# An adaLN, H3 and SwiGLU block: k's planes stored and loaded in order of use, first taps by halves, a quarter of the DFT matrix moved up

## The chip, the core and the metric

The kernel runs on one core of a Trainium2 chip. That core has a matrix engine (TensorE, PE; its weight loads are listed apart as PEld), three engines for elementwise work (VectorE or DVE, ScalarE or ACT, GpSimd or POOL), an engine that issues transfers (SyncE, SP), and 16 DMA engines that move data between the device memory and the on-chip memories. Each engine works through its own list of instructions in order and waits at an instruction until what it needs is there. The metric is the device time of one execution in microseconds (us).

## What is computed

One block with batch 1, S = 2048 tokens, D = 512 channels, F = 1792, all in float32. The core of the reference, shortened:

```python
mod = (silu(c) @ w_mod)            # six vectors sa, ca, ga, sb, cb, gb
h = layernorm(q) * (1 + ca) + sa
k_shift[t] = sum(k[t - i] * shift_k[:, i] for i in range(4))   # causal, per channel
kv = k_shift * v
y = irfft(rfft(pad(kv)) * rfft(pad(ssm_k)))[:S] + kv * ssm_D   # long causal convolution
x = q + ga * (h * y)
h = layernorm(x) * (1 + cb) + sb
out = x + gb * ((silu(h @ w_gate) * (h @ w_up)) @ w_down)
```

The change concerns only the first lines: how k, v and the DFT matrix come in, and how k_shift is made for the first two quarters of the channels.

## The kernel before

The channels are cut into four chunks of 128 (0 to 3). For every chunk the kernel makes kv = k_shift * v, transforms it and the filter ssm_k along time by a DFT of several steps (64 x 64 products with the matrix e_fwd, transposes of 32 x 32 blocks, small products with a matrix wc), multiplies the spectra and transforms back. This first stage takes about the first 125 us of the profile; behind it come the output products of the convolution, the norms, and then the SwiGLU part, which is matrix products on PE to the end.

The order of all work is written out by hand: a list of calls from line 1152 on, each of which appends its instructions to the engines that it names; instructions stay in that order on each engine, and the framework adds the waits. Tiles come from numbered buffers: a string of digits per kind (SLOTS, line 52) says which buffer each allocation takes. "e8" are eight buffers of 128 x 2048 numbers, for k, v, filter and tap results and for the DFT matrix ("er", line 235); "ps" are four pairs of PSUM banks. A tile in a used buffer waits for the last readers of the old one. All loads go out on SP in the order of the calls. The framework has eight semaphores for them, taken in turn: a load waits until the load eight places ahead of it has landed.

What the steps of the text use:

- Chunk 0 takes a path of its own, so that PE has work soon. Its k comes as "planes", 19 blocks of 128 x 128: plane j holds tokens with remainder j - 3 modulo 16, channels on partitions, preceded by three shifted ones for the taps; 20 small numbers per partition (taps of all chunks, c) stand ahead of them in the same tile (load_k0, line 163). The load has two pieces: the small numbers and planes 0 to 10 (714 KB), and planes 11 to 18 (512 KB).
- Chunk 0's first half of the tokens: four diagonal matrices of the taps (diag, line 180, "dg") are multiplied with the planes on PE (x0_taps, line 186, called for planes from 4 on and then from 0 on, planes 0 to 10 in all) and with v (x0_mul, line 196, DVE) into x00. Its second half: p_tap0 and p_tap (lines 204 and 208, DVE) make the taps on planes 8 to 18 elementwise into "u", p_mul (line 212, POOL and DVE) multiplies with v, and p_turn (line 216) transposes on PE; ACT copies the result into x01.
- Chunks 1 to 3 come with channels on partitions (load_k, load_v, lines 155 and 230). tap0 (line 243, ACT) makes the first tap of a whole chunk, tap (line 247, DVE) adds one of the other three, times_v (line 263) multiplies.
- load_e(q) (line 237) loads a quarter of the DFT matrix, x_first(c, q) (line 283) and k_first(c, q) (line 297) are the first products of chunk c with it: 8 matmuls, and a copy on ACT into X or kt. x_first(0, 0) and (0, 1) read x00, (0, 3) and (0, 2) read x01. swap_x and k_swap (DVE) transpose, x3 and product3 are the next products ("px" and "pk").
- warm(n) (line 136) runs n products on PE whose result nobody reads.

Of the kernel before, what the change touches and what calls it, by code (L numbers as in the profile page):

```python
# [42 lines left out]
def adaln_h3_swiglu(ctx, tc, q, k0, v0, kT, vT, ssm, dskip, wgu, wdn, wmod, e_fwd, e_inv, w_c, out):  # L43
# [8 lines left out]
    SLOTS = {  # L52
        "e8": "501234671063724603267137537135173135157137157137105637501657305617503657",
        "b16": "0123450224520214352",
# [99 lines left out]

    def load_k(b):
        kt = e8([P, S], F32, f"kt{b}")
        sp.dma_start(kt, kT[(b - 1) * P : b * P, :])
        kv[b] = [kt]

# [3 lines left out]
    def load_k0(h):  # L163

        if h == 0:
            t = head["t"] = b16("k0", (P, NS + (J + KS - 1) * P))
            head["k"] = t[:, NS:].rearrange("p (j m) -> p j m", m=P)
        m = NS + (J // 2 + KS - 1) * P
        r = slice(m, None) if h else slice(0, m)
        sp.dma_start(head["t"][:, r], k0[:, r])  # L170

    def load_v0(h):
        if h == 0:
            head["v"] = e8([P, 2, J // 2, P], F32, "v0")
        sp.dma_start(head["v"][:, h], v0[h])
# [4 lines left out]
    def diag(t, e=act):  # L180

        if t == 0:
            head["d"] = k2([P, KS, P], F32, "dg")
        scaled(e, head["d"][:, t], ident, head["t"][:, t : t + 1])

    def x0_taps(o):

        head["x", o] = bank("kvt")
        for jj in range(4):
            for t in range(KS):  # L190
                pe.matmul(
                    head["x", o][:, jj * P : (jj + 1) * P], head["k"][:, 4 * o + jj + KS - 1 - t],
                    head["d"][:, t], start=(t == 0), stop=(t == KS - 1),
                )
# [8 lines left out]

    def p_tap0(e=act):
        head["u"] = r4([P, J // 2, P], F32, "u0")
        scaled(e, head["u"], head["k"][:, J // 2 + KS - 1 :], head["t"][:, 0:1])

    def p_tap(t, h, e=dve):
        u, j = head["u"][:, 4 * h : 4 * h + 4], J // 2 + KS - 1 - t + 4 * h
        e.scalar_tensor_tensor(u, head["k"][:, j : j + 4], head["t"][:, t : t + 1], u, op0=ALU.mult, op1=ALU.add)  # L210
# [31 lines left out]

    def tap0(b, e=act):
        u = U[b] = e8([P, S], F32, f"u{b}")
        scaled(e, u, kv[b][0], shk_sb[:, b, 0:1])

    def tap(b, t):
        u = U[b]
        dve.scalar_tensor_tensor(
            u[:, t:], kv[b][0][:, : S - t], shk_sb[:, b, t : t + 1], u[:, t:], op0=ALU.mult, op1=ALU.add  # L250
        )

# [900 lines left out]
    load_k0(0)  # L1153
    load_k0(1)
    diag(0, e=act)
    diag(1, e=act)
    warm(7)
    diag(2, e=dve)
    small_in(e=act)
    silu_c()  # L1160
    load_k(1)
    p_tap0(e=dve)
    load_v0(0)
    p_tap(1, 0, e=dve)
    load_v0(1)
    load_k(2)
    load_dskip()
    p_tap(1, 1, e=dve)
    diag(3, e=act)
    x0_taps(1)  # L1170
    tap0(1, e=act)
    p_tap(2, 0, e=dve)
    p_tap(2, 1, e=dve)
    x0_taps(0)
    p_tap(3, 0, e=dve)
    p_tap(3, 1, e=dve)
    warm(5)
    tap(1, 1)
    tap0(2, e=act)
    x0_mul(0)  # L1180
    x0_mul(1)
    load_e(0)
    p_mul(0, e=pool)
# [575 lines left out]
```

## Time and profile before

| what | us |
|---|---|
| median of three runs (lowest, highest) | 566.36 (566.36, 566.46) |
| the profiled execution, its own time | 566.24 |
| span of that profile | 564.5 |
| busy: PE, PEld | 552.7, 431.1 |
| busy: DVE, ACT, POOL | 441.5, 288.7, 317.7 |

The profile is of one execution; its span runs from the first instruction to the last and is 1.74 us shorter than that execution's time. "Busy" counts instructions that run, not the waits. Names such as "kvt<-dg,k" mean: written tile, read tiles; "x64" is a count, and one product of float32 numbers is two matmul instructions. A bracket behind a row is the idle time of that engine just before it and what ended it. The chain of waits goes back from the last instruction, at each step to what released it; all else waited for something that was not last. Nearly every instruction has line 39, a helper, so rows are told apart by their tiles.

### The profile page before, as it was taken

To read this page: it belongs to the slowest core of one execution; us is meant where nothing else is said; L and a number is where in the kernel's file an instruction comes from. 1 tells how busy PE (TensorE), PEld (TensorE's weight loads), DVE (VectorE), ACT (ScalarE), POOL (GpSimd) and SP (SyncE) were. 2 spreads that over 40 slices of the span, in tenths; PEclk is the share of its full clock that TensorE was granted. 3 is DMA by queue.
4 is the path that set the end of the run, shared out by engine and by line. 5 is a ranking of instruction groups with operands and counts; after the bars stand their busy time and mean duration, and the time that the engine had idled before them with its cause. 6 is when DMAs were issued, how large, how long until landed. Compare 5 with 4: busy or idle time off the path is not lost.

```text
span 564.5 us, 9861 instructions
## 1 busy us (share of the span) xinstructions
PE 552.7 (98%) x3880; PEld 431.1 (76%) x3880; DVE 441.5 (78%) x602; ACT 288.7 (51%) x444; POOL 317.7 (56%) x298
## 2 busy tenths in 40 slices
PE   9899999898999999999999999999999999999997
PEld 9766456358788888888888888887888888888886
DVE  5989999998889666767567579858686868686766
ACT  3898889734664444434643556243434343434330
POOL 2359746899447966657978667550606061616110
PEclk9999999999999999999999999999999999999999
DMA  8998998991215655982897530544343434343304
GB/s 334 401 406 305 334 245 168 340 240 61 74 43 200 197 199 182 259 263 40 252 334 306 204 131 1 188 182 173 122 160 124 161 127 158 127 165 133 160 1 149
DMA packets 52544, 107.99 MB, mean 191 GB/s; under 512 B 19345, under 2 KB 34065, under 8 KB 46482
## 3 DMA queue, kind: packets, MB, share of 16 engines
q1 hardware_dynamic: 52498, 107.36, 56.3%
q8 instruction: 30, 0.49, 0.4%
q14 instruction: 16, 0.13, 0.1%
HBM read 72.74 MB, written 34.61 MB: 190 GB/s over the span
## 4 chain that ended last, share of the span: by engine, by line
PE 85%; DVE 9%; DMA 3%; ACT 1%; issue 1%; POOL 0%; SPq 0%; ACTq 0%; DVEq 0%
PE a L39 23%; PE dn L39 15%; PE c L39 12%; PE b L39 7%; PE da L39 6%; PE g L39 4%; PE s L39 4%; PE dc L39 3%; PE y L39 3%; DVE xs L39 3%; DVE X L39 2%; PE pk L39 2%; PE iv L39 2%; DMA er<-in_e_fwd 2%; DVE K L39 2%; PE px L39 1%
## 5 line engine op out<-in xcount | busy, mean ns | idle before, releaser
L39 PE MATMUL a<-op,wsum 128*128 128x512 f32 x432 | 109.9, 390 | 0.0
L39 PEld LDWEIGHTS a<-op,wsum 128*128 128x128 f32 x432 | 81.0, 188 | 17.5 <-ACT p L39 0.4
L39 PE MATMUL dn<-wd,acts 128*128 128x512 f32 x336 | 84.8, 389 | 0.0
L39 PEld LDWEIGHTS dn<-wd,acts 128*128 128x128 f32 x336 | 63.1, 188 | 13.1
L39 ACT COPY p<-a 128x512 f32<-128x512 f32 x50 | 29.4, 587 | 57.3 <-PE a L39 57.3
L39 DVE TENSOR_TENSOR x<-x,dn 128x512 f32<-128x512 f32 (+1 forms) x65 | 43.3, 671 | 13.2 <-PE dn L39 12.9
L39 POOL TENSOR_TENSOR wa<-ws,wa 128x512 fp32r<-128x512 f32 (+1 forms) x28 | 32.0, 1164 | 26.6 <-ACT wa L39 26.6
L39 POOL TENSOR_TENSOR tb<-wds 128x256 f32<-128x256 f32 x12 | 8.9, 744 | 62.4 <-DVE wds L39 62.4
L39 DVE TENSOR_TENSOR b<-r,c 128x512 f32<-128x512 f32 x24 | 16.7, 696 | 32.3 <-ACT sg L39 32.3
L39 ACT COPY r<-a 128x512 f32<-128x512 f32 x24 | 14.1, 587 | 53.7 <-PE a L39 53.6
L39 POOL TENSOR_TENSOR wsum<-sr,wsum 128x512 fp32r<-128x512 f32 x28 | 40.1, 1455 | 0.0
L39 PE MATMUL c<-op,wsum 128*128 128x512 f32 x156 | 39.6, 389 | 0.0
L39 PE MATMUL c<-op,wa 128*128 128x512 f32 x156 | 39.6, 389 | 0.0
L39 PE MATMUL b<-op,wa 128*128 128x512 f32 x144 | 36.5, 389 | 0.0
L39 POOL TENSOR_TENSOR wd<-wds,wd 128x512 fp32r<-128x512 f32 x14 | 18.3, 1329 | 30.4 <-ACT wd L39 30.4
L39 PEld LDWEIGHTS c<-op,wsum 128*128 128x128 f32 x156 | 29.3, 188 | 6.1
L39 PEld LDWEIGHTS c<-op,wa 128*128 128x128 f32 x156 | 29.3, 188 | 6.1
L39 POOL TENSOR_TENSOR s<-s,bcs 128x512 f32<-128x512 f32 x26 | 32.9, 1284 | 1.0
L39 DVE TENSOR_TENSOR x<-x,da 128x512 f32<-128x512 f32 x48 | 32.7, 681 | 0.9 <-PE da L39 0.9
L39 PEld LDWEIGHTS b<-op,wa 128*128 128x128 f32 x144 | 27.0, 188 | 5.6
L39 DVE TENSOR_TENSOR xs<-pk,xs 128x1024 f32<-128x1024 f32 x24 | 27.7, 1210 | 2.3 <-PE pk L39 2.2
L39 ACT ACTIVATE sg<-a 128x512 f32<-128x512 f32 x26 | 15.6, 599 | 22.5 <-PE a L39 22.5
(199 smaller groups left out, 1284.5 us busy)
## 6 DMA issues: line engine op xcount, KB each, us to landing
ds<-wsum SPq DMA_DIRECT2D x12, 1024.0 KB, 8.7
wsum<-ds SPq DMA_DIRECT2D x12, 1024.0 KB, 6.4
dw<-wa SPq DMA_DIRECT2D x12, 768.0 KB, 5.8
wa<-dw SPq DMA_DIRECT2D x12, 768.0 KB, 4.4
ws<-in_wgu SPq DMA_DIRECT2D x16, 512.0 KB, 4.3
wds<-in_wdn SPq DMA_DIRECT2D x14, 512.0 KB, 5.0
wm<-in_wmod SPq DMA_DIRECT2D x6, 1024.0 KB, 9.3
away<-X SPq DMA_DIRECT2D x3, 2048.0 KB
```

Of the source, the lines that this page charges most:

```text
L39: return lambda *a, **k: self.tc.keep_in_program_order(f(*a, **k))
```

## The change

Nothing is added to or taken from what is computed. Six things move.

1. k's planes are stored in another order: 8 to 18 first, then 0 to 7. The load has three pieces: the small numbers and planes 8 to 14 (458 KB), planes 15 to 18 (256 KB), planes 0 to 7 (512 KB). x0_taps finds its planes by a remainder.
2. p_tap0 makes its tap in two halves, and all taps of the first half run before those of the second. All four diagonals are now made on ACT.
3. Chunk 1's k comes in two halves; its tap0 and its first tap (1, 1) run by halves.
4. Both loads of chunk 1's k stand behind all pieces of k0, ahead of v0 as before.
5. load_e(0) is issued ahead of load_k(2) and load_dskip; it stood behind them.
6. tap0(2) stands behind x0_mul in the list, still ahead of the copy of x_first(0, 0) on ACT. The buffer numbers of "e8" are renamed to fit.

The diff:

```diff
-    def load_k(b):
-        kt = e8([P, S], F32, f"kt{b}")
-        sp.dma_start(kt, kT[(b - 1) * P : b * P, :])
-        kv[b] = [kt]
+    def part(h):
+        return slice(None) if h is None else slice(h * S // 2, (h + 1) * S // 2)
+
+    def load_k(b, h=None):
+        if not h:
+            kv[b] = [e8([P, S], F32, f"kt{b}")]
+        sp.dma_start(kv[b][0][:, part(h)], kT[(b - 1) * P : b * P, part(h)])
...
-        m = NS + (J // 2 + KS - 1) * P
-        r = slice(m, None) if h else slice(0, m)
+        m = [0] + [NS + n * P for n in (J // 4 + KS - 1, J // 2 + KS - 1, J + KS - 1)]
+        r = slice(m[h], m[h + 1])
         sp.dma_start(head["t"][:, r], k0[:, r])
...
-                    head["x", o][:, jj * P : (jj + 1) * P], head["k"][:, 4 * o + jj + KS - 1 - t],
+                    head["x", o][:, jj * P : (jj + 1) * P], head["k"][:, (4 * o + jj + KS - 1 - t - J // 2) % (J + KS - 1)],
...
-    def p_tap0(e=act):
-        head["u"] = r4([P, J // 2, P], F32, "u0")
-        scaled(e, head["u"], head["k"][:, J // 2 + KS - 1 :], head["t"][:, 0:1])
+    def p_tap0(h, e=act):
+        if h == 0:
+            head["u"] = r4([P, J // 2, P], F32, "u0")
+        j = KS - 1 + 4 * h
+        scaled(e, head["u"][:, 4 * h : 4 * h + 4], head["k"][:, j : j + 4], head["t"][:, 0:1])
...
-    def tap0(b, e=act):
-        u = U[b] = e8([P, S], F32, f"u{b}")
-        scaled(e, u, kv[b][0], shk_sb[:, b, 0:1])
+    def tap0(b, h=None, e=act):
+        if not h:
+            U[b] = e8([P, S], F32, f"u{b}")
+        scaled(e, U[b][:, part(h)], kv[b][0][:, part(h)], shk_sb[:, b, 0:1])
...
     warm(5)
     load_k0(0)
     load_k0(1)
+    load_k0(2)
     diag(0, e=act)
     diag(1, e=act)
     warm(7)
-    diag(2, e=dve)
+    p_tap0(0, e=dve)
+    diag(2, e=act)
+    diag(3, e=act)
+    load_k(1, 0)
+    load_k(1, 1)
+    p_tap(1, 0, e=dve)
+    p_tap(2, 0, e=dve)
+    p_tap(3, 0, e=dve)
+    load_v0(0)
+    load_v0(1)
     small_in(e=act)
     silu_c()
-    load_k(1)
-    p_tap0(e=dve)
-    load_v0(0)
-    p_tap(1, 0, e=dve)
-    load_v0(1)
+    p_tap0(1, e=dve)
+    p_tap(1, 1, e=dve)
+    x0_taps(1)
+    load_e(0)
     load_k(2)
     load_dskip()
-    p_tap(1, 1, e=dve)
-    diag(3, e=act)
-    x0_taps(1)
-    tap0(1, e=act)
-    p_tap(2, 0, e=dve)
+    tap0(1, 0, e=act)
     p_tap(2, 1, e=dve)
+    p_tap(3, 1, e=dve)
+    tap0(1, 1, e=act)
     x0_taps(0)
-    p_tap(3, 0, e=dve)
-    p_tap(3, 1, e=dve)
     warm(5)
-    tap(1, 1)
-    tap0(2, e=act)
+    tap(1, 1, 0)
+    tap(1, 1, 1)
     x0_mul(0)
     x0_mul(1)
-    load_e(0)
+    tap0(2, e=act)
     p_mul(0, e=pool)
```

On SP, the loads from the start to chunk 1's v (vt); kt is k of a chunk, ss the filter, bcs the row ssm_D. DMAHW0 to DMAHW7 are the eight semaphores of the loads in turn. Before:

```order
L39 DMA kt_119<-in_kT 128x2048
L39 DMA v_123<-in_v 128x1024 x2
L39 DMA kt_127<-in_kT 128x2048
L39 DMA bcs<-in_dskip 1x512
L39 DMA er<-in_e_fwd 128x512
L39 DMA ss_200<-in_ssm 128x512 [waits DMAHW0_49]
L39 DMA er<-in_e_fwd 128x512 [waits DMAHW1_49]
L39 DMA er<-in_e_fwd 128x512 [waits DMAHW2_49]
L39 DMA ss_200<-in_ssm 128x512 [waits DMAHW3_49]
L39 DMA er<-in_e_fwd 128x512 [waits DMAHW4_49]
L39 DMA vt_230<-in_vT 128x2048 [waits DMAHW5_49]
```

And in the changed kernel:

```order
L39 DMA kt_121<-in_kT 128x1024 x2
L39 DMA v_127<-in_v 128x1024 x2
L39 DMA er<-in_e_fwd 128x512
L39 DMA kt_152<-in_kT 128x2048 [waits DMAHW0_49]
L39 DMA bcs<-in_dskip 1x512 [waits DMAHW1_49]
L39 DMA ss_205<-in_ssm 128x512 [waits DMAHW2_49]
L39 DMA er<-in_e_fwd 128x512 [waits DMAHW3_49]
L39 DMA er<-in_e_fwd 128x512 [waits DMAHW4_49]
L39 DMA ss_205<-in_ssm 128x512 [waits DMAHW5_49]
L39 DMA er<-in_e_fwd 128x512 [waits DMAHW6_49]
L39 DMA vt_235<-in_vT 128x2048 [waits DMAHW7_49]
```

The first quarter (er) has passed chunk 2's k (the 128x2048 kt); the other quarters, which are those of x_first(0, 3), (0, 1) and (0, 2) in this order, keep their places. Chunk 2's k now waits for the first piece of k0 to land.

On DVE, from the start to the x0 products (x) and the second tap of chunk 1. Before:

```order
L39 TENSOR_SCALAR dg<-ident,k_102 128x128
L39 TENSOR_SCALAR u_121<-k_102 128x1024
L39 SCALAR_TENSOR_TENSOR u_121<-k_102,u_121 128x512 x6
L39 SCALAR_TENSOR_TENSOR u_149<-kt_119,sm,u_149 128x2047
L39 TENSOR_TENSOR x_181<-kvt,v_123 128x512 x2
L39 TENSOR_TENSOR v_123<-u_121,v_123 128x512
L39 SCALAR_TENSOR_TENSOR u_149<-kt_119,sm,u_149 128x2046
```

And in the changed kernel:

```order
L39 TENSOR_SCALAR u_117<-k_102 128x512
L39 SCALAR_TENSOR_TENSOR u_117<-k_102,u_117 128x512 x3
L39 TENSOR_SCALAR u_117<-k_102 128x512
L39 SCALAR_TENSOR_TENSOR u_117<-k_102,u_117 128x512 x3
L39 SCALAR_TENSOR_TENSOR u_155<-kt_121,sm,u_155 128x1023
L39 SCALAR_TENSOR_TENSOR u_155<-kt_121,sm,u_155 128x1024
L39 TENSOR_TENSOR x_185<-kvt,v_127 128x512 x2
L39 TENSOR_TENSOR v_127<-u_117,v_127 128x512
L39 SCALAR_TENSOR_TENSOR u_155<-kt_121,sm,u_155 128x2046
```

The diagonal is gone from DVE, the taps of chunk 0 are two groups of four, and the first tap of chunk 1 is two instructions; what follows is as before.

On PE, the first products of the taps (kvt) and, behind the warm products, the first one with the DFT matrix (s), with their waits. Before:

```order
L39 MATMUL kvt_132<-dg_105,k0_102 128x128 [waits DMAHW0_49,Activation_49]
L39 MATMUL kvt_132<-dg_105,k0_102 128x128 [waits Activation_49]
L39 MATMUL kvt_132<-dg_105,k0_102 128x128 [waits DVE_49]
L39 MATMUL kvt_132<-dg_105,k0_102 128x128 [waits Activation_49]
L39 MATMUL kvt_132<-dg_105,k0_102 128x128 x12
```

And in the changed kernel:

```order
L39 MATMUL kvt_134<-dg_106,k0_102 128x128 [waits DMAHW2_49,Activation_49]
L39 MATMUL kvt_134<-dg_106,k0_102 128x128 [waits Activation_49] x3
L39 MATMUL kvt_134<-dg_106,k0_102 128x128 [waits DMAHW0_49]
L39 MATMUL kvt_134<-dg_106,k0_102 128x128 x11
L39 MATMUL kvt_160<-dg_106,k0_102 128x128 x16
```

The first product waits for the third load (the last piece of k0) where it waited for the first.

More of the change, by code (lines that the diff above doesn't have):

```diff
@@ L52, in adaln_h3_swiglu @@
     SLOTS = {
-        "e8": "501234671063724603267137537135173135157137157137105637501657305617503657",
+        "e8": "201345671064735604367147247142174124147127147127104627401647204617402647",
         "b16": "0123450224520214352",
@@ L202, in x0_mul @@
         )
-    def p_tap0(e=act):
-        head["u"] = r4([P, J // 2, P], F32, "u0")
-        scaled(e, head["u"], head["k"][:, J // 2 + KS - 1 :], head["t"][:, 0:1])
+    def p_tap0(h, e=act):
[3 more added lines that the diff above has]
+        scaled(e, head["u"][:, 4 * h : 4 * h + 4], head["k"][:, j : j + 4], head["t"][:, 0:1])
     def p_tap(t, h, e=dve):
-        u, j = head["u"][:, 4 * h : 4 * h + 4], J // 2 + KS - 1 - t + 4 * h
+        u, j = head["u"][:, 4 * h : 4 * h + 4], KS - 1 - t + 4 * h
         e.scalar_tensor_tensor(u, head["k"][:, j : j + 4], head["t"][:, t : t + 1], u, op0=ALU.mult, op1=ALU.add)
@@ L241, in adaln_h3_swiglu, with tap @@
     U = {}
-    def tap0(b, e=act):
-        u = U[b] = e8([P, S], F32, f"u{b}")
-        scaled(e, u, kv[b][0], shk_sb[:, b, 0:1])
[L247 to L251, printed above, removed]
+    def tap0(b, h=None, e=act):
+        if not h:
+            U[b] = e8([P, S], F32, f"u{b}")
+        scaled(e, U[b][:, part(h)], kv[b][0][:, part(h)], shk_sb[:, b, 0:1])
+    def tap(b, t, h=None):
+        a, z = (0, S) if h is None else (h * S // 2, (h + 1) * S // 2)
+        u, k = U[b][:, max(a, t) : z], kv[b][0][:, max(a, t) - t : z - t]
+        dve.scalar_tensor_tensor(u, k, shk_sb[:, b, t : t + 1], u, op0=ALU.mult, op1=ALU.add)
     TM = {}
@@ L1718, in planes @@
         return x[at].transpose(3, 0, 1, 2).reshape(P, J + n, P)
+    k0 = planes(a(A_k)[0, :, :P], KS - 1)
+    k0 = np.concatenate([k0[:, J // 2 :], k0[:, : J // 2]], 1).reshape(P, -1)
     small = np.concatenate([
@@ L1727 @@
         "q": tokens(a(A_q)),
-        "k0": np.concatenate([small, planes(a(A_k)[0, :, :P], KS - 1).reshape(P, -1)], 1),
+        "k0": np.concatenate([small, k0], 1),
         "v0": np.stack([
```

## The prediction

> **What bounds the kernel now.** I read the chain of work that ended last first, then the windows, then each engine in order of time over the first 40 us, since all edits lie before 20 us.
>
> The chain in order of time; the columns are start, length and what the time went to.
>
> ```profile
> 1.63 7.25 DMA kt<-in_kT
> ...
> 8.90 9.26 DMA er<-in_e_fwd
> ...
> 18.20 6.66 PE s L39 x112
> 24.86 1.10 PE kvt L39 x8
> 25.96 2.73 PE px L39 x48
> 28.69 1.10 PE kvt L39 x8
> 29.80 6.45 PE s L39 x112
> 36.25 1.10 PE pk L39 x16
> ```
>
> From 18.2 to 37.35 the chain is TensorE without a gap. What starts it is the quarter of the DFT matrix (er) that x_first(0, 1) reads, issued at 8.90 and landed at 18.16. The piece ahead of it (kt) only says when that issue left SyncE. So the first question is what sets the landing at 18.16.
>
> Windows: length; busy time of PE, PEld, DVE, ACT and POOL; granted clock; DMA share; GB/s.
>
> ```profile
> 11.00:12.00 1.00, 1.00 (x12) 1.00 (x11) 1.00 (x2) 0.00 (x0) 0.42 (x1) 1.00 0.99 418
> ...
> 13.00:14.00 1.00, 1.00 (x12) 1.00 (x11) 1.00 (x3) 0.04 (x1) 1.00 (x1) 1.00 1.04 264
> 14.00:15.00 1.00, 0.37 (x4) 0.18 (x2) 1.00 (x2) 1.00 (x1) 0.52 (x1) 1.00 0.84 213
> ...
> 20.00:25.00 5.00, 5.00 (x87) 4.85 (x84) 4.86 (x4) 5.00 (x7) 2.84 (x3) 1.00 1.03 415
> 25.00:30.00 5.00, 5.00 (x68) 2.82 (x69) 5.00 (x4) 4.86 (x7) 3.08 (x3) 1.00 1.01 408
> 30.00:35.00 5.00, 5.00 (x94) 5.00 (x94) 5.00 (x5) 4.97 (x6) 3.05 (x3) 1.00 1.03 428
> ```
>
> The DMA engines are busy all the time, at 418 GB/s before 12 us. Between 13 and 15 they are as busy but move only 264 + 213 = 477 KB where 2 x 418 = 836 would pass: 359 KB, or 359/418 = 0.86 us, are lost there. A landing is thus set by the bytes queued ahead of it and by this slow stretch, not by when it was issued. From 20 to 35 us PE is full and ACT works 14.83 of 15 us: a matmul group needs a bank that ACT has emptied, so a delay of either one is handed on to 37 us.
>
> The engines that the edits touch (start, length, operation; the bracket is the idle time ahead and what ended it).
>
> ```profile
> 5.94 7.31 PE L39 MATMUL kvt<-dg,k 128*128 128x128 f32 x64
> 15.39 1.16 PE L39 MATMUL s<-x,er 64*128 64x128 f32 x16 [1.02 <-DMA er<-in_e_fwd]
> 18.20 2.95 PE L39 MATMUL s<-x,er 64*128 64x128 f32 x48 [0.63 <-DMA er<-in_e_fwd]
> 25.89 2.81 PE L39 MATMUL px<-X,wc 64*32 64x512 f32 x48
> ```
>
> ```profile
> 5.09 0.70 ACT L39 ACTIVATE dg<-ident,k 128x128 f32<-128x128 f32 x2 [2.88 <-DMA k<-in_k]
> 8.90 2.00 ACT L39 ACTIVATE u<-kt,sm 128x2048 f32<-128x2048 f32 x1 [2.49 <-DMA kt<-in_kT]
> 13.96 2.00 ACT L39 ACTIVATE u<-kt,sm 128x2048 f32<-128x2048 f32 x1 [3.05 <-DMA kt<-in_kT]
> 16.58 1.01 ACT L39 COPY X<-s 128x1024 f32<-128x1024 f32 x1 [0.62 <-PE s L39]
> ...
> 17.69 1.02 ACT L39 COPY x<-kvt 128x1024 f32<-128x1024 f32 x1
> 19.41 2.84 ACT L39 COPY X<-s 128x1024 f32<-128x1024 f32 x3 [0.70 <-PE s L39]
> ```
>
> ```profile
> 6.27 0.75 DVE L39 TENSOR_SCALAR u<-k 128x1024 f32<-128x1024 f32 x1 [0.88 <-DMA k<-in_k]
> 7.06 4.07 DVE L39 SCALAR_TENSOR_TENSOR u<-k,u 128x512 f32<-128x512 f32 x6
> 11.04 2.35 DVE L39 SCALAR_TENSOR_TENSOR u<-kt,sm,u 128x2047 f32<-128x2047 f32 x1
> 13.30 1.28 DVE L39 TENSOR_TENSOR x<-kvt,v 128x512 f32<-128x512 f32 x2
> 22.29 4.62 DVE L39 STREAM_TRANSPOSE X<-X 128x1024 f32<-128x1024 f32 x4
> 33.60 2.31 DVE L39 SCALAR_TENSOR_TENSOR u<-kt,sm,u 128x2045 f32<-128x2045 f32 x1
> 37.44 3.49 DVE L39 TENSOR_TENSOR xs<-pk,xs 128x1024 f32<-128x1024 f32 x3 [1.53 <-PE pk L39]
> ```
>
> DVE is not the bound here: at 35.91 it has nothing left and waits 1.53 us for PE. Two points have little cover. The second x_first group at 18.2 reads x01, which ACT finishes at 17.69 + 1.02 = 18.71; PE comes to it at 18.20 + 2.95/3 = 19.18, 0.47 later. And the third px group, at 25.89 + 2 x 2.81/3 = 27.76, reads what DVE's transposes finish at 26.91, 0.85 earlier.
>
> **The change part by part.** The issues of SyncE, each but the first held until the DMA eight places ahead of it has landed.
>
> ```profile
> 4.24 0.36 SPq L39 DMA_DIRECT2D er<-in_e_fwd  x1
> ...
> 8.90 0.33 SPq L39 DMA_DIRECT2D er<-in_e_fwd  x1
> 10.19 0.33 SPq L39 DMA_DIRECT2D ss<-in_ssm  x1
> 11.46 0.33 SPq L39 DMA_DIRECT2D er<-in_e_fwd  x1
> 13.96 0.33 SPq L39 DMA_DIRECT2D vt<-in_vT  x1
> ```
>
> By that rule chunk 1's k landed at 8.90, the halves of v at 10.19 and 11.46, chunk 2's k at 13.96.
>
> *More pieces.* There are two DMAs more (k's third piece, chunk 1's second half). Two 512 KB loads took 1.29 + 1.27 = 2.56 us, one of 1 MB took 13.96 - 11.46 = 2.50: a cut costs 0.06 us of queue. Two cuts cost **0.12 us**, paid by every later landing, the one at 18.16 among them; below, the cost is nothing. Their two issues (0.3 to 0.4 us each) stand ahead of loads that wait in the queue anyway; if the queue ran dry they would count in full.
>
> [...]
>
> *The quarter sooner.* load_e(0) passes chunk 2's k. The bytes ahead of the quarter at 18.16 stay the same, so that landing moves by the 0.12 us alone. If the slow stretch belonged to the old order and went, it would come up to 0.86 us sooner; a longer stretch would make it later by as much as it grows. I take no change, since the same small loads stay queued together. The quarter itself lands near 11.46 + 0.63 = 12.1 to 12.9. That ends the 1.02 us wait at 15.39, but PE then does only x_first(0, 0) and p_turn earlier and stands again before 18.2. What it wins there is nothing.
>
> *Chunk 2's k behind it.* The price is between 256 KB at 418 GB/s, 0.63 us, and the time the quarter needed itself, 15.39 - 13.96 = 1.43. ACT's order is tap0(2), copy of X, crep, copy of x01. Without the 0.62 us wait at 16.58, x01 is ready 2.00 + (17.69 - 16.58) + 1.02 = 4.13 us after chunk 2's k has landed. With 13.96 + 0.12 + 0.63 = 14.71 that is 18.84, still before 19.18; with 1.43 it is 19.64, and PE would lose 0.46. I take the lower end, because at 12 us the queue runs at 418 GB/s: **nothing**, with 0.34 us of cover left.
>
> *First taps by halves, on DVE.* A diagonal of 0.29 us leaves DVE and joins three others on ACT, which is done long before its next load. The taps start when 458 KB instead of 714 have landed, 256/418 = 0.6 us sooner, and the 0.88 us wait at 6.27 goes. Work of 0.75 + 4.07 + 2.35 us is cut into more instructions but hardly grows (512 columns cost 0.68 us, 2047 cost 2.35), so DVE arrives at the x0 product at about 11.8, not 13.30; chunk 1's halves on ACT (8.90 + 1.0 at the latest) do not hold it. But PE's x0 matmuls now read planes of the third piece. That has the place of the old second one, which DVE waited for until 6.27, so they start at about 6.4 in place of 5.94, and 7.31 us later the product starts at **13.75, 0.45 later than before**. What is late next is therefore PE, and the 1.5 us that DVE wins are idle. The 0.45 us runs on through DVE: transposes end at 27.36 (px at 27.76 covers it by 0.4), the last tap at 36.36 (PE at 37.44 covers it by 1.1). Cost at the end: nothing. If the third piece came over 0.4 us later still, each further us would count.
>
> *Chunk 1's load by halves.* ACT's first half starts near 7.6; both are done by 9.95 in place of 10.90. Nothing reads it sooner than DVE does, so this gives nothing.
>
> **Sum.** 0.12 + 0 + 0 + 0 = 0.1 us on the chain at 18.2. The profiled execution took 566.24 (span 564.5 and 1.74 around it), the median of the runs is 566.36; added to the median this is **566.5**.
>
> **The rivals.**
>
> *Slower: ACT becomes the bound at 19.2.* Chunk 2's k lands after 15.05, from where each us delays x01 past 19.18 and with it PE and ACT up to 37 us. For it: ACT has only 0.47 us of cover there. Against: 0.63 us at the running rate. With the quarter's own 1.43 it is 0.46 + 0.12 = 0.6; with the lost 0.86 us ahead of chunk 2's k as well, 1.4. I put it at 567.0, within 566.7 to 567.8.
>
> *Faster: the slow stretch shrinks.* The quarter at 18.16 comes up to 0.86 sooner, but the second group still needs x01, ready at 18.84 less what chunk 2's k wins too. PE gains about 0.5: 565.9. In no case more than 1.53 - 0.45 = 1.1 us on this path, since DVE is then the bound at 37.4: 565.3.
>
> *A cut load costs much more.* A 256 KB quarter took 1.43 where its bytes need 0.63. If that 0.8 is a price of each DMA, two cost 1.6: 568.0. Against it stand the 0.06 above.
>
> *The change does not do what it says.* It does, by the order of the issues; that it buys nothing is the forecast itself.
>
> **How the numbers follow.** Forecast 0.6, ACT 0.22, slow stretch 0.14, cut loads 0.04. About 0.2% (1.1 us) is what a measurement of this kernel tells from no change. Slower than 567.5 are the cut loads and a fifth of the ACT case: 0.08. Faster than 565.2 lies outside the cap of this path, so it must come from a coupling behind 37 us that I do not see; I leave it 0.1 of the chance, out of the forecast and the slow stretch. The rest, 0.82, is no change. The range, 565.4 to 567.3, takes in the slow stretch down to its cap and most of the ACT case.
>
> **What would show it.** Right: x_first(0, 0) starts near 14.9, the x0 product near 13.75 after an idle DVE, the three x_first groups near 18.3 on the DMA of er, pk near 36.3. Wrong: the groups interrupted near 19.2 by ACT (the ACT rival), a start near 17.5 (the slow stretch), or the third piece of k well later than 6.4 us. A difference that first shows after 40 us would mean that the couplings there, not these sums, decide.

## The result: slower, and the profile after

The changed kernel took 569.3 us (median of 8 runs, 567.47 to 573.21) against 566.41 (565.93 to 567.41): a ratio of 1.0064, 95% interval 1.0043 to 1.0084. The profiled execution took 569.88, its span is 568.1 (before 564.5), and its mean clock is 0.997 (before 1.000).

The chain that ended last, after (start, length, what), which answers to the first fence of the prediction:

```profile
4.63 12.67 DMA kt<-in_kT
...
17.32 2.00 ACT u L39
19.32 0.90 ACT X L39
20.22 0.20 ACT crep L39
20.41 0.92 ACT x L39
...
21.38 7.26 PE s L39 x96
28.64 1.10 PE kvt L39 x8
29.74 2.74 PE px L39 x48
32.48 1.10 PE kvt L39 x8
33.58 6.45 PE s L39 x112
40.03 1.10 PE pk L39 x16
```

TensorE's gapless part begins at 21.38 now, and what starts it is no longer a quarter of the DFT matrix but chunk 2's k: it lands at 17.30, and ACT's tap0(2) and three copies behind it run on to x01. At pk the kernel is 40.03 - 36.25 = 3.78 us late; from there the distance stays nearly the same to the end (568.1 - 564.5 = 3.6). Note also the group of 96 at 21.38: in the profile before, 112 products of the same kind took 6.66.

The engines in order of time, after:

```profile
6.40 7.38 PE L39 MATMUL kvt<-dg,k 128*128 128x128 f32 x64 [0.47 <-DMA k<-in_k]
14.82 1.16 PE L39 MATMUL s<-x,er 64*128 64x128 f32 x16
19.21 1.16 PE L39 MATMUL s<-x,er 64*128 64x128 f32 x16 [2.20 <-DMA er<-in_e_fwd]
21.38 3.38 PE L39 MATMUL s<-x,er 64*128 64x128 f32 x32 [1.01 <-ACT x L39]
```

```profile
13.82 1.29 DVE L39 TENSOR_TENSOR x<-kvt,v 128x512 f32<-128x512 f32 x2 [0.99 <-PE kvt L39]
9.11 2.39 ACT L39 ACTIVATE u<-kt,sm 128x1024 f32<-128x1024 f32 x2 [3.07 <-DMA kt<-in_kT]
17.32 2.00 ACT L39 ACTIVATE u<-kt,sm 128x2048 f32<-128x2048 f32 x1 [5.81 <-DMA kt<-in_kT]
20.32 1.01 ACT L39 COPY x<-kvt 128x1024 f32<-128x1024 f32 x1
41.22 1.22 DVE L39 TENSOR_TENSOR xs<-pk,xs 128x1024 f32<-128x1024 f32 x1 [1.76 <-PE pk L39]
```

PE waits 2.20 us for er and, one group later, 1.01 us for x01. The 32 products at 21.38 take 3.38 us, where two groups of 16 took 2 x 2.95/3 = 1.97 before. The windows say why; the column after POOL is the granted clock, the last one GB/s:

```profile
18.00:19.00 1.00, 0.00 (x0) 0.00 (x0) 1.00 (x2) 1.00 (x1) 0.00 (x0) 1.00 1.04 412
...
21.00:22.00 1.00, 0.62 (x10) 0.62 (x12) 1.00 (x1) 1.00 (x2) 0.00 (x0) 0.94 1.03 386
22.00:23.00 1.00, 1.00 (x12) 1.00 (x12) 0.70 (x1) 0.25 (x1) 0.00 (x0) 0.50 1.10 428
...
24.00:25.00 1.00, 1.00 (x14) 1.00 (x14) 0.00 (x0) 0.31 (x2) 1.00 (x2) 0.50 1.03 426
25.00:26.00 1.00, 1.00 (x18) 1.00 (x18) 0.15 (x1) 0.81 (x1) 1.00 (x2) 0.86 0.96 401
```

The clock is half for 0.12 + 3 + 0.28 = 3.4 us from about 21.9; the trace's own record of the clock says 3.413, from 21.87. Its stretches at full clock are whole multiples of that length: 17.067 us ahead of the half (5 x 3.4133), 542.719 behind it (159), and 559.786 in before (164); below, one such step is a window of the clock. From 22 to 23 us 12 products began, where before 24 of the same kind began from 20 to 21, so half speed for that long loses an estimated 1.7 us; below this is called a lost window. So the 3.78 us at pk are 19.21 - 18.20 = 1.0 (er later), 1.0 (x01 later) and 1.7 (clock): 3.7.

The same windows where the loads run slow, and SyncE's issues behind them:

```profile
5.00:6.00 1.00, 0.93 (x9) 0.73 (x7) 0.96 (x2) 0.97 (x5) 0.00 (x0) 1.00 1.17 287
6.00:7.00 1.00, 0.60 (x5) 0.64 (x6) 0.96 (x2) 0.04 (x1) 0.00 (x0) 1.00 0.76 197
7.00:8.00 1.00, 1.00 (x11) 1.00 (x10) 0.96 (x3) 0.00 (x0) 0.00 (x0) 1.00 0.90 295
```

```profile
12.94 0.33 SPq L39 DMA_DIRECT2D er<-in_e_fwd  x1
13.58 0.33 SPq L39 DMA_DIRECT2D vt<-in_vT  x1
...
17.31 0.80 SPq L39 DMA_DIRECT2D ss<-in_ssm  x2
```

The slow stretch has moved: 779 KB in the three windows where 3 x 418 = 1254 would pass, so 475/418 = 1.14 us are lost at 5 to 8 us, on chunk 1's halves. Before, 0.86 us were lost at 13 to 15 us, on the first quarter of er, *behind* chunk 2's k. Now the stretch stands *ahead* of it. (In its middle window the DMA engines' busy share is 0.76, so a part of the loss there is idle time of theirs.) The quarter landed at 13.56 (it releases the issue at 13.58), chunk 2's k at 17.30.

The record of the landings adds what no row shows: a load has sixteen, as many as there are DMA engines, and what waits for it here goes on after the last. Of chunk 2's k fifteen had come by 16.07 and the last at 17.29 (tap0(2) starts at 17.32); of the quarter that x_first(0, 1) reads, fifteen by 18.05 and the last at 19.16 (PE starts at 19.21). Before, that quarter had fifteen by 17.64 and the last at 18.16. So both waits of PE contain 1.1 to 1.2 us of one late landing; by the other fifteen the quarter is only 0.41 us later than before.

**One number for each run.** The record of every run gives the mean clock granted. 3.413 us at half is 1.7/566 = 0.3%: a mean of 1.000 or 0.999 is read as a run without a lost window, 0.996 or 0.997 as one with one, 0.993 or 0.994 as one with two. Of the 8 runs after, two lost none (567.5 and 568.3), four one (568.9 to 569.9), two two (572.9 and 573.2). Two windows alone are 3.4 us, so these last two must have been late by other things as well. Runs of before lose one too at times; the table counts them. Left out of the table's counts and full-clock medians are one run of r4_a_spread_warm (800.05 us) and two of before in the second group (1440.65 and 1440.74), far slower than all others, and one of before in the fourth (567.71 us at a mean clock of 0.948), which fits none of these readings.

### The profile page after: what moved, and what is told of

The parts are those of the page before. It is cut to its first block, busy times and chain, and to the rows that moved or that the text cites. A ratio compares the mean times of both kernels' runs of the same rounds, so it can differ in the third digit from the quotient of the medians.

```text
span 568.1 us, 9866 instructions
## 1 busy us (share of the span) xinstructions
PE 554.4 (98%) x3880; PEld 432.6 (76%) x3880; DVE 441.9 (78%) x603; ACT 289.3 (51%) x446; POOL 315.4 (56%) x298
## 4 chain that ended last, share of the span: by engine, by line
PE 85%; DVE 9%; DMA 2%; ACT 2%; issue 1%; SPq 1%; POOL 0%; ACTq 0%; DVEq 0%
PE a L39 23%; PE dn L39 15%; PE c L39 12%; PE b L39 6%; PE da L39 6%; PE g L39 4%; PE s L39 4%; PE dc L39 3%; PE y L39 3%; DVE xs L39 3%; DMA kt<-in_kT 2%; DVE X L39 2%; PE pk L39 2%; PE iv L39 2%; DVE K L39 2%; PE px L39 1%
## 5 line engine op out<-in xcount | busy, mean ns | idle before, releaser
L39 DVE TENSOR_TENSOR x<-x,dn 128x512 f32<-128x512 f32 (+1 forms) x65 | 43.2, 670 | 13.2 <-PE dn L39 12.9
L39 ACT ACTIVATE sg<-a 128x512 f32<-128x512 f32 x26 | 15.6, 600 | 22.4 <-PE a L39 22.4
```

What stands on the lines that cost most here:

```text
L39: return lambda *a, **k: self.tc.keep_in_program_order(f(*a, **k))
```

## The experiments

The runs come in four groups, each with runs of the kernel before on the same chip; the first ran on one chip, the second on another, the third and fourth on a third. "Full clock": runs without a lost window, their number and median, and how far that is above the same of the kernel before in the same group. "Lost": runs with a window lost or more. The last three columns are from each kernel's one profile: start of the first products of chunk 0 (in the changed order they also need k's last piece), of tap0(2) (waits for chunk 2's k) and of x_first(0, 1) (needs er; in r1_warm_gap, r2_b_k1_halves, r3_b_fill and r4_a_spread_warm PE was busy until it began, so that there the column does not give the landing).

| kernel | full clock | lost | ratio, interval | kvt | tap0(2) | x_first |
|---|---|---|---|---|---|---|
| before, groups 1, 2, 3, 4 | 29, 24, 24, 20: 566.3 to 566.4 | 6, 9, 11, 13 | | 5.94 | 13.96 | 18.20 |
| r1_again | 4: 567.2 (+0.8) | 8 | 1.0038, 1.0021 to 1.0055 | 7.20 | 16.04 | 18.88 |
| r1_e_back | 5: 566.9 (+0.5) | 7 | 1.0024, 1.0008 to 1.0041 | 6.55 | 15.24 | 18.86 |
| r1_k1_whole | 7: 567.1 (+0.7) | 5 | 1.0019, 1.0006 to 1.0032 | 7.00 | 16.11 | 18.81 |
| r1_warm_gap | 7: 567.5 (+1.1) | 5 | 1.0025, 1.0013 to 1.0038 | 6.62 | 16.00 | 19.32 |
| r2_tap0_late | 6: 567.05 (+0.7) | 6 | 1.0024, 1.0007 to 1.0042 | 6.46 | moved | 19.76 |
| r2_b_e_first | 4: 566.5 (+0.1) | 8 | 1.0028, 1.0007 to 1.0050 | 6.62 | 15.40 | 18.27 |
| r2_b_k1_halves | 8: 566.7 (+0.3) | 4 | 1.0013, 0.9993 to 1.0034 | 5.90 | 14.48 | 18.77 |
| r2_b_contig | 11: 566.1 (-0.3) | 1 | 0.9991, 0.9978 to 1.0003 | 5.96 | 13.90 | 17.75 |
| r3_a_contig | 9: 566.8 (+0.5) | 3 | 1.0012, 0.9997 to 1.0027 | 7.50 | 15.63 | 18.60 |
| r3_b_fill | 8: 567.05 (+0.8) | 4 | 1.0012, 1.0000 to 1.0024 | 6.53 | 13.84 | 17.00 |
| r3_b_swap | 9: 566.25 (0.0) | 3 | 0.9995, 0.9983 to 1.0007 | 5.77 | 13.86 | 17.17 |
| r3_b_swap_fill | 9: 566.5 (+0.2) | 2 | 0.9999, 0.9987 to 1.0011 | 6.27 | 13.87 | 17.31 |
| r4_b_spread | 12: 566.4 (0.0) | 0 | 0.9986, 0.9975 to 0.9998 | 6.00 | 13.75 | 18.02 |
| r4_a_spread | 6: 567.4 (+1.1) | 6 | 1.0021, 1.0006 to 1.0036 | 6.50 | 16.14 | 18.99 |
| r4_a_spread_warm | 10: 568.1 (+1.8) | 1 | 1.0024, 1.0010 to 1.0038 | 8.20 | 16.53 | 22.16 |
| r4_best | 10: 566.2 (-0.2) | 2 | 0.9989, 0.9976 to 1.0002 | 6.17 | 13.59 | 17.79 |

### Parts undone, and the gap filled (first group)

r1_again is the changed kernel as it is.

> The changed kernel once more, for its own spread. Its first profile had chunk 2's k landing at 17.3 us, x01 ready at 21.3, the clock at half from 21.9 to 25.3. If all three belong to the change: 568 to 570 us, chunk 2's k landing within 0.5 us of 17.3. If the slow stretch of the DMA engines at 5.5 to 7.5 us was chance: it lies elsewhere or is gone, and chunk 2's k lands at 15 to 16.

r1_e_back puts the quarter behind chunk 2's k again:

```diff
-    load_e(0)
     load_k(2)
     load_dskip()
+    load_e(0)
```

> The changed kernel with the first quarter of the DFT matrix issued behind chunk 2's k and the row ssm_D again; all else as changed. Order theory (the quarter ahead of chunk 2's k makes ACT late): chunk 2's k lands 0.6 us sooner, near 16.7, x01 at 20.7, 0.6 us gained, and 2.3 if the clock then stays up (567.0). Strided theory (halves of chunk 1's k cost the DMA time): still above 568.5.

r1_k1_whole loads chunk 1's k in one piece:

```diff
-    load_k(1, 0)
-    load_k(1, 1)
+    load_k(1)
```

> The changed kernel with chunk 1's k in one load again (the taps stay in halves). Strided theory: the slow stretch at 5.5 to 7.5 us goes, chunk 2's k lands near 15.8, 1.5 us gained and the clock stays up: about 567.0. Order theory: chunk 2's k still near 17, still 568.5 to 570.

r1_warm_gap puts eight unused products into PE's gap ahead of x_first(0, 1):

```diff
     p_turn(e=act)
     tap(1, 3)
+    warm(8)
     x_first(0, 1, e=act)
```

> The changed kernel with eight more warm products on PE between p_turn and x_first(0, 1), in the gap at 17.0 to 19.2 us. Clock theory (the idle gap halves the clock for 3.4 us, worth about 1.7): clock 1.0, the x_first group with x01 still starts near 21.4, 567.5 to 568. If the late x01 alone costs the time: no change, 569 to 570.

Measured: the loss stays on another chip (1.0038, where it was 1.0064; the intervals overlap). Without lost windows the changed kernel is only 0.8 us above before; 8 of 12 runs lost windows. Neither undone part brings it all back, and with medians of 568.24 (r1_e_back) and 567.83 (r1_k1_whole) neither meets the numbers of one of its two theories; by the overlap of the intervals it is open how much either gains. In r1_again chunk 2's k came at 16.04 and not near 17.3, in r1_e_back at 15.24: with the slow stretch on chunk 1's halves in both (160 GB/s at 6 to 7 us of r1_again; the first half was there at 9.05 in it and at 8.95 in r1_e_back), the quarter ahead costs it 0.80. In r1_k1_whole the slow stretch was gone from 5 to 8 us (chunk 1's k was whole by 9.38, where its second half landed at 10.33 in after) and stood at 11 to 12 (236 GB/s), on the quarter of er, which there is ahead of chunk 2's k too: 16.11. A cut load costs nothing that shows: 567.2 with two halves, 567.1 with one. Filling the gap has a price: in r1_warm_gap er had landed at 18.65, but the unused products held PE until 19.32. With the gap filled no run lost two windows (2 of 12 in r1_again), but five lost one; its profile shows where, in a second gap that all these kernels have:

```profile
143.00:144.00 1.00, 0.48 (x2) 0.30 (x2) 1.00 (x5) 1.00 (x2) 1.00 (x2) 1.00 0.04 12
144.00:145.00 1.00, 1.00 (x4) 0.78 (x3) 0.96 (x7) 0.97 (x3) 0.90 (x2) 0.53 0.78 217
145.00:146.00 1.00, 1.00 (x4) 0.81 (x3) 1.00 (x1) 0.58 (x2) 0.99 (x1) 0.50 0.97 393
```

### Single steps, and the slow stretch taken away (second group)

r2_tap0_late is the changed kernel with tap0(2) behind the copies on ACT:

```diff
-    tap0(2, e=act)
     ...
     p_turn(e=act)
+    tap0(2, e=act)
```

> The changed kernel with chunk 2's first tap moved on ACT behind p_turn's copy, its copy into X and crep's copy; nothing else. Theory A (chunk 2's k lands at 15.2 to 17.3 us and its 2.00 us tap, queued ahead of the copy of x01, holds TensorE up): the copy of x01 ends near 18.5 to 19.0 whatever chunk 2's k does, the three x_first groups are ended in their wait by the DMA of er alone (18.8 to 19.2) and run on without a wait for ACT; about 0.2 to 0.8 us less than the changed kernel. DVE's taps of chunk 2 then start about 2 us later, and pay only if they reach past 36 us. Theory B (the clock): a gap of TensorE before er stays, of about 2 us, but without the second one of 1.0; so the half clock at the head should not come, and runs of a mean clock under 0.995 should be gone. Rival (the base loss of 0.7 us comes from er's last quarter alone, 18.8 in place of 18.2): no gain, 567.0 to 567.6 at full clock.

r2_b_e_first and r2_b_k1_halves are the kernel before with one step of the change each:

```diff
+    load_e(0)
     load_k(2)
     load_dskip()
     ...
-    load_e(0)
```

> The kernel before with load_e(0) put ahead of chunk 2's k and dskip, alone: one step of the change. If the slow stretch belongs to the first load that takes part of every row, it lies on this quarter at about 11 to 13 us, chunk 2's k lands near 15.2 to 15.6 in place of 13.96, the copy of x01 ends near 19.4 to 19.8 and TensorE waits for ACT by 0.2 to 0.6 us: 566.6 to 567.2 at full clock. If chunk 2's k lands near 14.7, as the prediction had it, x01 is done before er and the time is that of before within 0.2 us. If order alone is the loss of the change, this kernel has all of it (567.5 and more).

```diff
-        sp.dma_start(kt, kT[(b - 1) * P : b * P, :])
+        for r in ((slice(0, S // 2), slice(S // 2, S)) if b == 1 else (slice(0, S),)):
+            sp.dma_start(kt[:, r], kT[(b - 1) * P : b * P, r])
```

> The kernel before with chunk 1's k loaded in two halves of every row, alone; the taps unchanged. If the slow stretch belongs to the first load that takes part of every row, it moves onto the first half, at 5 to 8 us, with packets of 4096 bytes at 300 to 700 ns in place of 159; the second half lands 0.3 to 1 us later than chunk 1's k did (8.90), and the quarter that took 1.43 us takes about 0.65; all in all the landing of er's last quarter moves by less than 0.3 us. If it belongs to the time (12.7 to 14.7) or to the quarter itself, it stays there. The time: within 0.4 us of before either way.

r2_b_contig is the kernel before with the pieces of the DFT matrix and of chunk 0's filter stored one behind the other, so that a piece is one stretch of memory and not a part of every row:

```diff
-            sp.dma_start(raw[:, 4 * jq : 4 * jq + 4], e_fwd[:, 4 * jq : 4 * jq + 4])
+            sp.dma_start(raw[:, 4 * jq : 4 * jq + 4], e_fwd[jq])
-            sp.dma_start(SS[c_][:, 4 * jq : 4 * jq + 4], ssm[:, c_, 4 * jq : 4 * jq + 4])
+            sp.dma_start(SS[c_][:, 4 * jq : 4 * jq + 4], ssm0[jq])
```

> The kernel before with the DFT matrix and chunk 0's filter stored as four contiguous quarters each, so that no early load reads part of a row; same loads, same order. If the slow stretch comes from part-row reads, it goes: no packets over 150 ns at 12.7 to 14.8 us, the quarter lands 0.6 to 0.7 us behind chunk 2's k, er's last quarter near 17.3 in place of 18.16, and the kernel gains 0.4 to 0.6 us, until the copy of x01 (18.7) is late next. If it comes from something else (a first touch of that memory, a coincidence of two queues), packets stay slow at about the same time and the time stays within 0.2 us of before.

The windows with the lowest rates, first of r2_b_e_first, then of r2_b_k1_halves, then 13 to 15 us of r2_b_contig:

```profile
11.00:12.00 1.00, 1.00 (x12) 1.00 (x11) 1.00 (x1) 0.00 (x0) 0.76 (x1) 1.00 0.88 262
```

```profile
6.00:7.00 1.00, 1.00 (x11) 1.00 (x10) 0.69 (x1) 0.45 (x2) 0.00 (x0) 1.00 1.05 242
7.00:8.00 1.00, 1.00 (x11) 1.00 (x11) 0.96 (x3) 0.00 (x0) 0.00 (x0) 1.00 0.87 307
```

```profile
13.00:14.00 1.00, 1.00 (x12) 1.00 (x11) 1.00 (x3) 0.10 (x1) 1.00 (x1) 1.00 1.03 389
14.00:15.00 1.00, 0.68 (x9) 0.52 (x8) 1.00 (x2) 1.00 (x1) 0.45 (x1) 1.00 1.09 391
```

Each of the two steps alone draws the slow stretch to its own load, to 11 us (262 GB/s) and to 6 us (242). With the pieces of r2_b_contig it is gone: 389 and 391 GB/s where before had 264 and 213. That kernel's three x_first groups start 0.45 sooner:

```profile
17.75 2.95 PE L39 MATMUL s<-x,er 64*128 64x128 f32 x48 [0.86 <-DMA er<-in_e_fwd]
```

It gained 0.3 us at full clock, less than the 0.4 to 0.6 expected (and the interval of its ratio takes in 1), because er landed at 17.7 and not at 17.3: the landing records show 15 of its 16 landings by 16.55 and the last at 17.71, and the record of the packets has an instruction packet of 16 KB that took 1.10 us at 14.75. Every profile has such a packet between 14.3 and 18.7 us, 0.94 to 1.13 us long (before 0.94 at 15.45, after 1.08 at 15.12). That the late landing is that of the engine which carries the packet is an inference from the times; the records do not name the engine. In r2_b_k1_halves fifteen landings of er's first quarter had come by 15.10, 0.64 us after chunk 2's k and as expected, and the sixteenth at 16.52, behind a packet of 1.11 us at 14.35.

In r2_tap0_late the rival held: the wait for ACT went, but er came at 19.76 (fifteen landings by 18.64), and at 567.05 nothing that shows was won over the changed kernel:

```profile
19.76 2.95 PE L39 MATMUL s<-x,er 64*128 64x128 f32 x48 [2.69 <-DMA er<-in_e_fwd]
```

Six of its runs lost windows as before. The profiled one did not, though its gap is 2.69 us long: by the boundaries of the clock record 1.57 us of it fell into one window and 1.12 into the next (they meet at 18.64).

The steps price chunk 2's k: the quarter ahead +1.44 (13.96 to 15.40), the halves of chunk 1 +0.52; together 1.96, near the 2.08 of r1_again. At full clock each alone costs only 0.1 and 0.3 us; that both draw on the same 0.47 us of cover fits, but was not tested. And r2_b_e_first has only four runs at full clock: eight of 12 lost a window, and its ratio, 1.0028, is not far from the 1.0038 of the whole change. Why it lost so many was not seen; its profile has no long gap at the head (0.67 us).

### The changed kernel with its pieces stored, and first tries against the clock (third group)

r3_a_contig is the changed kernel with chunk 1's halves, the DFT matrix and chunk 0's filter stored piece by piece (the lines for the last two are those of r2_b_contig):

```diff
-        sp.dma_start(kv[b][0][:, part(h)], kT[(b - 1) * P : b * P, part(h)])
+        sp.dma_start(kv[b][0][:, part(h)], kT[(b - 1) * P : b * P] if h is None else kT1[h])
```

> The changed kernel, loads and order as they are, with chunk 1's k, the DFT matrix and chunk 0's filter stored so that each piece it loads lies in one stretch of memory. If the slow stretch of the loads is what the prediction missed, chunk 2's k lands near 14.7 to 15.0 (the 14.71 of the prediction, later by the instruction fetch at most), er's last piece near 17.7 to 18.0, the copy of x01 ends at 18.8 to 19.1, and the time at full clock is 566.0 to 566.6, 0.5 to 1.0 us under the changed kernel; TensorE's gap before er falls under 1.2 us, so runs of a mean clock under 0.995 go. If the order of the loads itself is the cause (a quarter more ahead of chunk 2's k), chunk 2's k still lands after 15.2 and the time stays at 567.0 to 567.6.

r3_b_fill is the kernel before with one call of transposes done twice; r3_b_swap is r2_b_contig with two quarters of er exchanged; r3_b_swap_fill has both:

```diff
     norm_t(0, 1)
+    norm_t(0, 1)
```

> The kernel before with the second four of the transposes at 138.5 us (norm_t) done twice, which fills 0.54 us of TensorE's 1.54 us gap at 139.6; the same values are written again. If lost clock windows come from windows with about half of their time idle, the gaps of 1.0 + 0.54 us are then too short, and the runs of before at a mean clock of 0.996 to 0.997 (9 of 33, about 1.7 us longer) go: 0 or 1 of 12, the fast ones unchanged at 565.9 to 566.6. If the lost windows are chance and have nothing to do with the gap, 3 of 12 stay. ACT's second activation there starts at 140.35 and the transposes end at about 140.1, so the repeat delays nothing.

```diff
     load_ssm(0, 0)
-    load_e(3)
+    load_e(1)
     ...
-    load_e(1)
+    load_e(3)
```

> The kernel before with the DFT matrix and chunk 0's filter stored piece by piece (as in the run that lost the slow stretch), and besides the quarter that x_first(0, 1) reads loaded one place earlier, ahead of the quarter of x_first(0, 3). TensorE would start that group at 17.0 to 17.2, behind p_turn, in place of 17.75; the second group needs the copy of x01 (18.03) only at 18.2. So pk comes 0.6 to 0.7 us sooner, near 36.4, unless DVE's last tap there is later (36.4 to 36.8): 565.3 to 565.9 at full clock, against 565.5 to 566.1 without the swap. If DVE holds pk, no gain.

> The last kernel and the repeated transposes together. If both hold: the fast times of that one, 565.3 to 565.9, with 0 or 1 of 12 runs below a mean clock of 0.998, so a median about 1 us under that of before, and the interval of the ratio wholly under 1.

r3_a_contig missed its number: chunk 2's k came at 15.63, though the two-window losses went (3 of 12 lost one) and 0.5 us over before are left of 0.8 to 1.1. Its stretch is smaller but not gone (295 and 356 GB/s at 5 to 7 us). So storing the quarters piece by piece took it away from the kernel before (389 and 391 GB/s at 13 to 15 us); where chunk 1's k comes in halves, stored in the same way, it was only lessened (after has 287 and 197 at 5 to 7 us). r3_b_fill failed by its own mechanism:

```profile
138.73 1.53 PE L39 MATMUL nt<-ident,n 128*128 128x128 f32 x12
141.80 1.09 PE L39 MATMUL nt<-ident,n 128*128 128x128 f32 x8 [1.54 <-ACT hraw L39]
```

The gap is as long as before, only later: ACT reads the tile after its last write (its first hraw starts at 140.29 in place of 139.62), so the repeat delayed all behind it (+0.8 us) and says nothing on the clock. The exchange of r3_b_swap brought x_first to 17.17, but pk did not follow (xs at 37.10 against 37.01 in r2_b_contig), and its 566.25 missed the 565.3 to 565.9 expected. The chain now runs over ACT's copies of X and kt up to 22.4, so ACT is the next bound on this path:

```profile
22.46 2.06 PE L39 MATMUL s<-ss,er 64*128 64x128 f32 x32 [0.24 <-ACT kt L39]
```

r3_b_swap_fill, with both, missed too (566.5, two of 11 runs lost a window).

### The later gap taken away (fourth group)

Sixteen products of y, which stood ahead of the transposes, go behind them, into the gap. The call at the old place now only takes their PSUM buffer; room(), which takes another buffer, moves along:

```diff
     def y_pe(t, *cs):
-        ps = banks("y").rearrange("p n (j d) -> p n j d", j=4)
+        if (t, cs) not in Y:
+            Y[t, cs] = banks("y").rearrange("p n (j d) -> p n j d", j=4)
+            if (t, cs) == (2, (0, 1)):
+                return
+        ps = Y[t, cs]
...
-        Y[t, cs] = ps
...
-    room()
     norm1(0, 0, e=act)
...
     norm_t(0, 1)
+    y_pe(2, 0, 1)
+    room()
     norm_s(0, 0, e=act)
```

r4_b_spread is before with it, r4_a_spread the changed kernel, r4_a_spread_warm the changed kernel with warm(8) as well, r4_best is r2_b_contig with it.

> The kernel before with the last 16 products of y (0.98 us of TensorE, at 137.5 us) moved behind the first eight transposes nt, into the gap of 1.54 us that follows them; nothing added. No window of 3.41 us then has more than about 1.1 to 1.5 us idle after 100 us. Clock theory: no run at a mean clock of 0.997 or less (before: 9 of 33 and 11 of 35), the others unchanged, 565.7 to 566.9, so a median of 566.0 to 566.4. If the lost windows have nothing to do with that gap: 3 or 4 of 12 stay.

> The changed kernel with the same move. Clock theory: the losses of the later gap go, those of the gap at 17 to 21 us stay: no run with two windows lost (0.993, 0.994; before this move 4 of 20), 5 to 8 of 12 with one (0.996, 0.997) at 568.5 to 569.9, the rest at 567.0 to 568.0. If the gap at the head is harmless, no run is lost and all lie at 567.0 to 568.0.

> The last kernel with eight unused products (1 us) in the head's gap, ahead of x_first(0, 1). Clock theory: no run loses a window; all at 567.0 to 568.0, median 567.2 to 567.6, which is the price of the late data alone (0.8 to 1.2 us over before without lost windows). If the lost windows were not due to the gaps: as many lost as in the last kernel.

> The kernel before with the DFT matrix and chunk 0's filter stored piece by piece, and the same move of 16 products. If both hold, 565.4 to 566.2 in all runs and no window lost: a median near 565.8, against 566.5 to 567.0 of before, with the interval of the ratio wholly under 1. If the stored pieces gain nothing, the median is that of the first kernel of this call.

TensorE at that place, before and in r4_b_spread:

```profile
138.49 1.09 PE L39 MATMUL nt<-ident,n 128*128 128x128 f32 x8
141.12 1.09 PE L39 MATMUL nt<-ident,n 128*128 128x128 f32 x8 [1.54 <-ACT hraw L39]
```

```profile
138.08 1.43 PE L39 MATMUL nt<-ident,n 128*128 128x128 f32 x8 [1.13 <-ACT n L39]
139.44 1.97 PE L39 MATMUL y<-X,ei 128*64 128x128 f32 x32
141.34 1.09 PE L39 MATMUL nt<-ident,n 128*128 128x128 f32 x8
```

The wait is cut in two parts further from each other, no work is added, and lost windows go from 13 of 33 to 0 of 12 while the median at full clock stays at 566.4. In the changed kernel the move leaves the gap at the head alone: 6 of 12 lost exactly one window (568.5 to 570.0), none two. With the head filled 1 of 11 lost. So in these three kernels the gaps cause the lost windows. The time did not follow, though: the medians of all runs are 568.48 without and 568.42 with the filling, and at full clock 568.1 instead of the 567.2 to 567.6 expected. The profile of r4_a_spread_warm shows one thing more that the change costs:

```profile
8.20 9.01 PE L39 MATMUL kvt<-dg,k 128*128 128x128 f32 x64 [1.92 <-DMA k<-in_k]
```

```profile
9.00:10.00 1.00, 1.00 (x7) 1.00 (x7) 0.82 (x2) 0.46 (x1) 0.00 (x0) 0.50 1.07 438
10.00:11.00 1.00, 1.00 (x6) 1.00 (x6) 0.27 (x1) 0.89 (x2) 0.00 (x0) 0.50 1.00 410
```

k's third piece was complete at 8.1 (of its sixteen landings fifteen came by 6.39 and one at 8.06, while packets of chunk 1's first half took up to 1.17 us), and the idle 1.92 us were followed by a half clock of their own, 9.01 us for products that took 7.38. The eight unused products then stand in the way. Why the other runs of that kernel at full clock spread from 567.2 to 569.9 was not seen. r4_best is 0.5 us under before in the median; its interval just reaches 1, that of r4_b_spread does not. Two of its 12 runs lost a window, where none was expected; where, was not seen.

## Why the prediction was wrong

**The slow stretch** is the term that failed, and with it the step "Chunk 2's k behind it". The text said of it "I take no change, since the same small loads stay queued together", which left it behind chunk 2's k. So that k was to land at 14.71, at a cost of "nothing, with 0.34 us of cover left", and the landing at 18.16 was to move by 0.12 alone. In the runs the stretch goes with the first load that takes a part of every 8 KB row, and not with a place in the queue: 264 and 213 GB/s at 13 to 15 us of before and 262 at 11 to 12 of r2_b_e_first on er's first quarter, 197 at 6 to 7 of after and 242 of r2_b_k1_halves on chunk 1's first half. It moved to chunk 1's halves and so in front of chunk 2's k, and grew from 0.86 to 1.14 us. Chunk 2's k came at 17.30 in this profile, at 16.0 to 16.5 in four more of the changed order and at 17.71 in r2_tap0_late. 13.96 + 0.63 + 1.14 + 0.12 is 15.85, near the 16.0 to 16.5. The quarter's own 0.63 was nearly right (0.80 by r1_again less r1_e_back); the 1.43 that it had taken, and the 1.44 of r2_b_e_first, contain the stretch. The rest to 17.30 is the one late landing (fifteen by 16.07, the last at 17.29), which is in no step of the prediction. Chunk 1's halves, on ACT foretold done by 9.95, were done at 11.50 for the same reason.

**What it cost** went two ways. The text's own rival, "ACT becomes the bound at 19.2", with 15.05 as the point from which it decides, came true in this profile: PE waits 1.01 us for x01. But er itself came later too, by 1.0 us here and by 0.7 in r1_again, where the wait inside the three x_first groups adds only 0.3 (3.28 in place of 2.95). With ACT's tap out of the way (r2_tap0_late) no gain shows, because there er was late (19.76). So the rival named the right chain, and is only a part of the loss.

**The clock** is in no step of the prediction. All windows before 35 us showed 1.00, and the text took that for a constant. The two waits of 2.20 and 1.01 us, themselves the result of late data, were followed by half the clock for 3.4 us; without that this execution would have been an estimated 1.7 us shorter. That such gaps cause it is shown by the fourth group: 13 of 33 runs of before lost a window, 0 of 12 with its later gap broken up. The trace has the half clock as one stretch of 3.413 us; in the 3.413 us ahead of it, from 18.46 to 21.87, PE was idle for 1.76 (0.75 up to its start at 19.21, and the 1.01).

**"More pieces"**, 0.12 us for all later landings, was too small for er (18.16 before, 18.8 to 19.2 in the changed order; by fifteen landings 17.64 and 18.05, where 0.12 and the 0.28 by which the stretch grew make 0.40), though not for the reason of the rival: cutting itself costs nothing that shows (567.2 in r1_again, 567.1 in r1_k1_whole). That k's third piece could be held up by the loads behind it was named as a risk without a price ("If the third piece came over 0.4 us later still, each further us would count"); it starts PE at 6.40 here, at 7.20 in r1_again, at 8.20 in r4_a_spread_warm.

**Right** were the steps on DVE and PE up to 15 us: the x0 product at 13.82 (13.75 foretold) behind an idle DVE, kvt at 6.40 (6.4), x_first(0, 0) at 14.82 (14.9), and a DVE that waits for PE at pk (1.76 us). The quarter itself landed at 13.56, past the foretold 12.1 to 12.9.

Of the median loss of 2.9 us at least 0.8 to 1.5 are later data (567.2 and 567.9 at full clock against 566.4). The rest is not lost windows alone. The runs of r1_again with one lost window lie 2.2 to 3.6 us above its full clock, more than the 1.7 of a window, so the runs that lose one are likely those whose data came late; and r4_a_spread_warm, with hardly a window lost, is still 1.8 above before, its unused products included. In the profiled execution the split is 2.0 for data and 1.7 for the clock; over all runs it stays open, and so does the split within the data: the single steps give 0.1 and 0.3, which do not add up to the whole.

## What to carry to other kernels

Loads that are moved or cut can move a slow stretch too: here 0.86 us lost at 13 to 15 us became 1.14 at 5 to 8, on another load. So ask of every slow stretch in a profile whether it belongs to the place, to the load, or to the first load of its kind, and what will stand behind it afterwards. A wait of TensorE can cost more than its length: here 1.72, 1.76 and 1.92 us idle in one window of 3.413 were followed by half the clock for the next, an estimated 1.7 us. So gaps were worth breaking up: moving 16 products gave 0.14% (interval 0.02 to 0.25%) with nothing else changed. And compare runs by their granted clock before asking what the data cost, but remember that runs picked by their clock may be the ones whose data came early.

## What was not expected of the hardware

- The slow stretch fell on the first load that reads a part of every 8 KB row: on er's first quarter in before (213 GB/s in its slowest window), r2_b_e_first (262) and r1_k1_whole (236), on chunk 1's first half in after (197), r1_again (160), r2_b_k1_halves (242) and r4_a_spread_warm (201). In r2_b_contig, where all of these are stored as pieces, it is gone (389 and 391 GB/s at 13 to 15 us); in r3_b_swap, r3_b_swap_fill and r4_best, stored alike, x_first(0, 0), which needs er's first quarter, began at 14.65, 14.66 and 14.53 without a wait for it, where before waited for it until 15.39. Its single packets of 4 KB took up to 1.9 us where 0.16 is usual (r1_again; 1.48 in after). What does it was not tried. Parts of rows alone do not: the pieces of k0 are parts of rows of 9,808 bytes, and the windows from 3 to 5 us of before ran at 391 and 414 GB/s. A fifth kernel stored so, r3_a_contig, keeps a part of it (295 and 356 GB/s at 5 to 7 us) though it loads no part of a row of these. It also varies: in r3_b_fill, with the loads of before, it is smaller (274 and 324 GB/s at 13 to 15 us) and er's first quarter kept nobody waiting.
- A window of 3.413 us with 1.72 us idle was followed by a lost one (r1_warm_gap), one with 1.76 too (after), and one with 1.92 (r4_a_spread_warm); the clock record gives each lost one as 3.413. In r4_a_spread a gap of 1.88, of which 1.80 fell into one window by the record's boundaries, was not, nor the 1.57 and 1.12 in r2_tap0_late. From when on idle time costs the clock these numbers do not settle: 1.80 without a loss stands against 1.72 and 1.76 with one, and the ends of the products are modelled.
- One landing of sixteen came late by about 1.1 us behind a packet of instructions (16 KB, 0.94 to 1.13 us, in every profile), and so did that of each load that was under way: fifteen by 16.07 and one at 17.29, fifteen by 18.05 and one at 19.16 (after), by 16.55 and 17.71 (r2_b_contig); before, by 17.64 and 18.16, it was 0.5. That it is one DMA engine, the packet's, is inferred from the times.
